# Rebuilding phase one of a fused scan-and-attention kernel: fused rotations, carry on GpSimd, sums on TensorE, V ahead, states in x's memory

## The chip, the cores and the metric

The kernel runs on one core of a Trainium2 chip. The metric is device time in microseconds (us); lower is better. An execution is called slow if it takes more than 1.5% longer than the fastest one of the same kernel. A profiled execution gives a trace whose span is about 1.7 us shorter than the time of the same run. Times below are medians of runs; spans and waits come from the one profiled execution.

Engine names as in the profile: PE is TensorE (PEld its weight loads), DVE is VectorE, ACT is ScalarE, POOL is GpSimd, SP is SyncE, which here mainly issues DMAs. The suffix q (SPq, ACTq) marks a DMA issued from that engine. PSUM is the memory into which the matmuls here write; evacuation is the copying of a finished result out of it. The granted clock is the share of TensorE's full clock that the profile shows; a half-clock window is a stretch in which it is 0.5.

## The reference

Two independent computations on 2048 tokens of 1024 values, whose results stand side by side in the output.

```python
# A: a complex diagonal state space model (1024 states)
Lam_bar = exp(dt * Lam);  B_bar = ((Lam_bar - 1) / Lam)[:, None] * Bmat
Bu = einsum('bld,pd->blp', x, B_bar)
for t in range(L):  h = Lam_bar * h + Bu[:, t, :]          # states h, kept for every t
y = 2 * einsum('blp,dp->bld', hseq, Cmat).real + x * Dskip
# B: attention in 64 segments of 32 tokens, 32 heads of 128, with 8 memory rows
for s in range(n_seg):
    h = concatenate([mem, x[segment s]])
    q, k, v = h @ Wq, h @ Wk, h @ Wv
    o = softmax(mask(q k^T * scale)) v;   o = o @ Wo
    mem = o[:8];  out(o[8:])
return concatenate([y, out], -1)
```

The kernel evaluates B from a guess of the memory rows. The guess needs the sum of x over each segment.

## The kernel before

Phase one goes through 8 chunks (`pc`) of 128 states and, for each, four quarters (`tb`) of 512 tokens. Each quarter has 32 matmuls of the projection V = x Wv (`v_x`) and 16 matmuls of B x (`stage1`), all with 512 columns. The scan is made real by rotating the products by a table of cosines and sines, scanning real and imaginary part separately, and rotating back. The states go to DRAM (`a_hs`). Phase two multiplies the states by C (`stage2`) and computes the memory guess. Phase three is attention and its output projection.

```python
def stage1(self, pc, tb):
    tcp, tsp, tc2, ts2 = self.tabs
    ur = k.ps("S"); ui = k.ps("O")
    for i, u in enumerate((ur, ui)):
        for c in range(KC):
            PE.matmul(u[:], self.bt[:, i, c, :], self.xT[:, c, tb * TB:(tb + 1) * TB], start=(c == 0), stop=(c == KC - 1))
    # rotation: six VectorE operations on 512 columns
    V.tensor_tensor(wr[:], ur[:], c_, ALU.mult)
    V.tensor_tensor(ta[:], ui[:], s_, ALU.mult)
    V.tensor_tensor(wr[:], wr[:], ta[:], ALU.add)
    # ... the same three for wi
    V.tensor_tensor_scan(wr[:], rb, wr[:], 0.0 if ini is None else ini[:, 0:1], ALU.mult, ALU.add)
    V.tensor_tensor_scan(wi[:], rb, wi[:], 0.0 if ini is None else ini[:, 1:2], ALU.mult, ALU.add)
    if tb < NB - 1:      # carry to the next quarter: four VectorE operations on one column
        V.tensor_scalar(tt[:, 0:1], wi[:, TB - 1:TB], sT, None, ALU.mult)
        V.scalar_tensor_tensor(nx[:, 0:1], wr[:, TB - 1:TB], cT, tt[:, 0:1], ALU.mult, ALU.subtract)
        # ... the same two for nx[:, 1:2]
    S.activation(gr[:], wr[:], ACT.Copy); S.activation(gi[:], wi[:], ACT.Copy)
    # rotation back: six bf16 VectorE operations, into h
    k.SP.dma_start(self.hs[tb][:, pc, :, :], h[:])

def sum_x(self):         # segment sums on VectorE
    # ... for pieces of the transposed x:
    k.V.tensor_reduce(self.xsum[...], self.xe[...].rearrange("p c (s n) -> p c s n", n=SEG), AX.X, ALU.add)

def v_x(self, hb, w):
    # ... 8 matmuls into a PSUM tile, copied by ScalarE to the staging tile st (b_vst, 2 buffers)
    k.SP.dma_start(vx[s0:s0 + n * 128, :]..., st[:, 0:n, :, :]...)

def load_c(self, q):     # called in chunks 4 to 7
    for i, w in enumerate((self.Cre, self.Cim)):
        self.k.SP.dma_start_transpose(self.CT[:, i, :, cols], w[cols, :])

# main loop of phase one
for pc in range(PC):
    v = b.v_x(pc, wv)
    for tb in range(NB):
        # ... in chunk 0: V first, and the next quarters of x loaded
        a.stage1(pc, tb)
        # ... tb == 2: tables and B weights of the next chunk
        # ... pc > 0: four steps of V;  pc >= 1: two steps of sum_x
    if pc >= 2:
        b.og(pc, wv)     # needs the sums; 32 matmuls of 64 columns
# phase two: stage2 loads the states (a_hl) into memory taken after phase one,
#   guess(), and at its very end v_mem(0), v_mem(1): memory rows of V

def qk_init(self, pool): # start of phase three: zero the padding of two pairs of q and k tiles
    for i in range(2):
        # ... three V.memset for each of q and k
```

A scheduler orders the instructions of each engine; a DMA is free to be moved ahead unless it is pinned with `keep_in_program_order`.

Of the kernel before, what the change touches and what calls it, by code (L numbers as in the profile page):

```python
# [51 lines left out]
class K:  # L52
    def __init__(self, tc, ctx):
        self.tc, self.nc = tc, tc.nc
        nc = tc.nc
        self.V, self.G, self.S, self.PE, self.SP = nc.vector, nc.gpsimd, nc.scalar, nc.tensor, nc.sync
        self.cst = ctx.enter_context(tc.tile_pool(name="cst", bufs=1, side="left"))
        self.psp = ctx.enter_context(tc.tile_pool(name="ps", bufs=1, space=PSUM))
        self.drp = ctx.enter_context(tc.tile_pool(name="dr", bufs=1, space=DRAM))

    def ps(self, tag, shape=(128, 512), dt=FP32):
        return self.psp.tile(list(shape), dt, name="ps" + tag, bufs={"P": 3, "S": 2, "R": 1, "O": 2}[tag])
# [8 lines left out]
def consts(k):  # L71
# [6 lines left out]
    k.ones = c.tile([128, 128], BF16, name="ones")  # L78
    V.memset(k.ones[:], 1.0)
    k.hpb = c.tile([128, 1], FP32, name="hpb")  # L80
    V.memset(k.hpb[:], HALF_PI)

# [43 lines left out]
class PartA:  # L126
# [6 lines left out]
    def params(self, pool, tmp):  # L133
# [45 lines left out]
        ji = tmp.tile([128, TB + 1], I32, name="a_k1")  # L179
# [3 lines left out]
    def tables(self, pc):  # L183
        k = self.k; V, S = k.V, k.S
        tp, tb = self.tmp, self.tab
        turn, bre, bim, jf = self.turn, self.bre, self.bim, self.jf
        q = pc % 2
        tcp = tb.tile([128, TB + 1], FP32, name=f"a_tabc{q}", bufs=1); tsp = tb.tile([128, TB + 1], FP32, name=f"a_tabs{q}", bufs=1)
        tc2 = tb.tile([128, TB], BF16, name=f"a_tabd{q}", bufs=1); ts2 = tb.tile([128, TB], BF16, name=f"a_tabe{q}", bufs=1)
        k1 = tp.tile([128, TB + 1], FP32, name="a_k1")  # L190
        V.tensor_scalar(k1[:], jf[:], turn[:, pc:pc + 1], MAGIC, ALU.mult, ALU.add)
        V.tensor_scalar(k1[:], k1[:], MAGIC, None, ALU.subtract)
        fr = tp.tile([128, TB + 1], FP32, name="a_fr")
        V.scalar_tensor_tensor(fr[:], jf[:], turn[:, pc:pc + 1], k1[:], ALU.mult, ALU.subtract)
        S.activation(tsp[:], fr[:], ACT.Sin, scale=TWO_PI_LO)
        V.scalar_tensor_tensor(k1[:], fr[:], -1.0, fr[:], ALU.mult, ALU.max)
        S.activation(tcp[:], k1[:], ACT.Sin, scale=-TWO_PI_LO, bias=k.hpb[:])
        t1 = tp.tile([128, TB + 1], FP32, name="a_k1")
        S.activation(t1[:, 0:TB], tsp[:, 0:TB], ACT.Copy, scale=bim[:, pc:pc + 1])
        V.scalar_tensor_tensor(tc2[:], tcp[:, 0:TB], bre[:, pc:pc + 1], t1[:, 0:TB], ALU.mult, ALU.subtract)  # L200
        t2 = tp.tile([128, TB + 1], FP32, name="a_fr")
        S.activation(t2[:, 0:TB], tcp[:, 0:TB], ACT.Copy, scale=self.nbim[:, pc:pc + 1])
        V.scalar_tensor_tensor(ts2[:], tsp[:, 0:TB], self.nbre[:, pc:pc + 1], t2[:, 0:TB], ALU.mult, ALU.add)
        self.tabs = (tcp, tsp, tc2, ts2)
# [10 lines left out]
    def load_c(self, q):  # L215

        cols = slice(q * 256, (q + 1) * 256)
        for i, w in enumerate((self.Cre, self.Cim)):
            self.k.SP.dma_start_transpose(self.CT[:, i, :, cols], w[cols, :])

    def stage1(self, pc, tb):
        k = self.k; V, S, PE = k.V, k.S, k.PE
        if tb == 0:
            self.carry = None
        tcp, tsp, tc2, ts2 = self.tabs
        ur = k.ps("S"); ui = k.ps("O")
        for i, u in enumerate((ur, ui)):
            for c in range(KC):
                PE.matmul(u[:], self.bt[:, i, c, :], self.xT[:, c, tb * TB:(tb + 1) * TB], start=(c == 0), stop=(c == KC - 1))  # L229
        c_, s_ = tcp[:, 0:TB], tsp[:, 0:TB]  # L230
        wr = self.wp.tile([128, TB], FP32, name="a_wr"); wi = self.wp.tile([128, TB], FP32, name="a_wi")
        ta = self.wp.tile([128, TB], FP32, name="a_ta", bufs=1)
        V.tensor_tensor(wr[:], ur[:], c_, ALU.mult)
        V.tensor_tensor(ta[:], ui[:], s_, ALU.mult)
        V.tensor_tensor(wr[:], wr[:], ta[:], ALU.add)
        V.tensor_tensor(wi[:], ui[:], c_, ALU.mult)
        V.tensor_tensor(ta[:], ur[:], s_, ALU.mult)
        V.tensor_tensor(wi[:], wi[:], ta[:], ALU.subtract)
        rb = self.rr[:, pc:pc + 1].to_broadcast([128, TB])
        ini = self.carry  # L240
        V.tensor_tensor_scan(wr[:], rb, wr[:], 0.0 if ini is None else ini[:, 0:1], ALU.mult, ALU.add)
        V.tensor_tensor_scan(wi[:], rb, wi[:], 0.0 if ini is None else ini[:, 1:2], ALU.mult, ALU.add)
        if tb < NB - 1:
            cT, sT = tcp[:, TB:TB + 1], tsp[:, TB:TB + 1]
            nx = self.wp.tile([128, 2], FP32, name="a_nx"); tt = self.wp.tile([128, 2], FP32, name="a_tt")
            V.tensor_scalar(tt[:, 0:1], wi[:, TB - 1:TB], sT, None, ALU.mult)
            V.scalar_tensor_tensor(nx[:, 0:1], wr[:, TB - 1:TB], cT, tt[:, 0:1], ALU.mult, ALU.subtract)
            V.tensor_scalar(tt[:, 1:2], wi[:, TB - 1:TB], cT, None, ALU.mult)
            V.scalar_tensor_tensor(nx[:, 1:2], wr[:, TB - 1:TB], sT, tt[:, 1:2], ALU.mult, ALU.add)
            self.carry = nx  # L250
        gr = self.wp.tile([128, TB], BF16, name="a_gr"); gi = self.wp.tile([128, TB], BF16, name="a_gi")
        S.activation(gr[:], wr[:], ACT.Copy); S.activation(gi[:], wi[:], ACT.Copy)

        h = self.wp.tile([128, 2, TB], BF16, name="a_h")
        n1 = self.wp.tile([128, TB], BF16, name="a_n1", bufs=1); n2 = self.wp.tile([128, TB], BF16, name="a_n2", bufs=1)
        V.tensor_tensor(n1[:], gr[:], tc2[:], ALU.mult)
        V.tensor_tensor(n2[:], gi[:], ts2[:], ALU.mult)
        V.tensor_tensor(h[:, 0, :], n1[:], n2[:], ALU.add)
        V.tensor_tensor(n1[:], gr[:], ts2[:], ALU.mult)
        V.tensor_tensor(n2[:], gi[:], tc2[:], ALU.mult)  # L260
        V.tensor_tensor(h[:, 1, :], n1[:], n2[:], ALU.subtract)
        k.SP.dma_start(self.hs[tb][:, pc, :, :], h[:])

    def stage2(self, pool):

        k = self.k; V, G, PE = k.V, k.G, k.PE
        q0 = k.G
        dB = pool.tile([128, D], BF16, name="a_dB", bufs=1)
        q0.dma_start(dB[:], self.Dskip.unsqueeze(0).to_broadcast([128, D]))
        xns = {}  # L270

        def load_xn(t, q):
            xns[t] = pool.tile([128, D], BF16, name="a_xn2", bufs=3)
            q.dma_start(xns[t][:], self.x[0][t * 128:(t + 1) * 128, :])
        for t in range(3):
            load_xn(t, q0)

        def load_h(tb, q0):
            hl = []
            for q in range(4):  # L280
                hl.append(pool.tile([128, 2, 2, TB], BF16, name=f"a_hl{q}", bufs=2))
                k.tc.keep_in_program_order(q0.dma_start(hl[q][:], self.hs[tb][:, 2 * q:2 * q + 2, :, :]))
            return hl
        nxt = load_h(0, q0)
        for tb in range(NB):
            hl = nxt
            for tt in range(4):
                t0 = tb * TB + tt * 128
                xn = xns.pop(4 * tb + tt)
                xd = pool.tile([128, D], FP32, name="a_xd", bufs=2)  # L290
                G.tensor_tensor(xd[:], xn[:], dB[:], ALU.mult)
                ot = pool.tile([128, D], BF16, name="a_ot", bufs=2)
                for half in range(2):
                    hs = slice(half * 512, (half + 1) * 512)
                    py = k.ps("O")
                    for pc in range(PC):
                        for i in range(2):
                            PE.matmul(py[:], hl[pc // 2][:, pc % 2, i, tt * 128:(tt + 1) * 128], self.CT[:, i, pc, hs],  # L298
# [3 lines left out]
                k.SP.dma_start(self.out[0, t0:t0 + 128, 0:D], ot[:])  # L302
                if 4 * tb + tt + 3 < TT:
                    load_xn(4 * tb + tt + 3, k.SP)
                if tt == 0 and tb + 1 < NB:
                    nxt = load_h(tb + 1, k.SP)
# [3 lines left out]
class PartB:  # L310
# [20 lines left out]
    def init(self, tmp):  # L331
        k = self.k
        k.V.memset(self.accE[:], 0.0)
        m0 = tmp.tile([M, D], BF16, name="b_m0", bufs=1)
# [9 lines left out]
        z = tmp.tile([32, 4 * EV], BF16, name="b_zero", bufs=1)  # L344
# [8 lines left out]
    def load_x(self, q):  # L353

        for t, c, n in self.chunks(q):
            step = 128 if q == 0 else n
            for o in range(0, n, step):
                self.k.SP.dma_start_transpose(self.xe[:, :, c + o:c + o + step], self.x[0][t + o:t + o + step, :])
# [7 lines left out]
    def sum_x(self):  # L366

        k = self.k
        for t, c, n in sum((self.chunks(q) for q in range(4)), []):
            m = 2 if n > 64 else KC  # L370
            for h in range(0, KC, m):
                k.V.tensor_reduce(self.xsum[:, h:h + m, t // SEG:(t + n) // SEG],
                                  self.xe[:, h:h + m, c:c + n].rearrange("p c (s n) -> p c s n", n=SEG), AX.X, ALU.add)
                yield

    def fin_xbar(self, tmp):
        k = self.k
        ms = tmp.tile([128, KC], FP32, name="b_ms", bufs=1)
        k.V.tensor_reduce(ms[:], self.m0T[:], AX.X, ALU.add)
        k.V.tensor_scalar(self.xbar[:], self.xsum[:], 1.0 / L, None, ALU.mult)  # L380
        k.V.tensor_tensor(ms[:], ms[:], self.xsum[:, :, 0], ALU.add)
        k.V.tensor_scalar(self.xbar[:, :, 0], ms[:], 1.0 / L, None, ALU.mult)

    def load_wv(self, hb):
# [655 lines left out]
```

## Time and profile before

| | before |
|---|---|
| device time, median (lowest to highest) | 1290.06 us (1287.63 to 1290.8), 3 runs |
| profiled span, mean granted clock | 1290.2 us, 0.994 |
| phase one / two / three, from the timeline of PE | 363.9 / 134.9 / 791.4 us |

The page begins with the span and the busy time of each engine, its share of the span and its instructions:

```profile
span 1290.2 us, 19225 instructions
PE 1252.3 (97%) x7698; PEld 649.9 (50%) x7698; DVE 716.2 (56%) x1611; ACT 250.7 (19%) x609; POOL 223.7 (17%) x340
```

TensorE is busy 97% of the time, so a faster kernel must win gaps and slow stretches. The share of VectorE, 56%, is an average over phases with different limits. The busy time of each engine in stretches of phase one, followed by the granted clock, the DMA share and GB/s, shows how near VectorE is to its limit:

```profile
60.00:150.00 90.00, 85.22 (x386) 37.74 (x384) 89.76 (x172) 32.93 (x58) 1.35 (x8) 0.99 0.66 161
150.00:250.00 100.00, 100.00 (x546) 46.80 (x545) 93.83 (x183) 37.74 (x67) 1.53 (x9) 1.00 0.41 114
```

The third figure after the length is VectorE: 89.76 us of 90, then 93.83 of 100. GpSimd, the fifth, is all but idle. What PE waits for (in all, how often, longest):

```profile
PE psP L400 <- DMA b_xe<-in_B_x_dram: 12.6, 4, 7.9
PE psP L400 <- ACT b_vst L66: 4.7, 6, 2.9
PE psO L298 <- DMA a_hl<-a_hs: 4.4, 2, 3.8
PE psO L298 <- DVE a_ot L300: 2.7, 3, 2.0
PE psO L563 <- DMA b_v<-b_vt: 2.0, 1, 2.0
```

The first line is the load of x at the start, the second VectorE's backlog in phase one (ScalarE's evacuation waits behind it), the third and fourth phase two, the last phase three. Some VectorE groups by shape, with count, busy time and mean ns:

```profile
L233 DVE TENSOR_TENSOR a_wr<-psS,a_tabc 128x512 f32<-128x512 f32 x32 | 22.0, 686 | 2.0 <-PE psS L229 1.5
L372 DVE TENSOR_REDUCE b_xsum<-b_xe 128x32 f32<-128x1024 bf16 x12 | 14.5, 1213 | 4.0 <-DMA b_xe<-in_B_x_dram 4.0
L256 DVE TENSOR_TENSOR a_n<-a_gr,a_tabd 128x512 bf16<-128x512 bf16 x32 | 12.8, 401 | 0.0
L247 DVE SCALAR_TENSOR_TENSOR a_nx<-a_wr,a_tabc,a_tt 128x1 f32<-128x1 f32 x24 | 5.2, 217 | 0.0
```

These are a multiply of the rotation (0.69 us), a piece of the segment sums (1.2 us), a multiply of the back-rotation (0.40 us) and an operation of the carry on one column (0.22 us; a carry has four, so 0.84 us).

### The profile page before, as it was taken

To read this page: it belongs to the slowest core of one execution; us is meant where nothing else is said; L and a number is where in the kernel's file an instruction comes from. 1 tells how busy PE (TensorE), PEld (TensorE's weight loads), DVE (VectorE), ACT (ScalarE), POOL (GpSimd) and SP (SyncE) were. 2 spreads that over 40 slices of the span, in tenths; PEclk is the share of its full clock that TensorE was granted. 3 is DMA by queue.
4 is the path that set the end of the run, shared out by engine and by line. 5 is a ranking of instruction groups with operands and counts; after the bars stand their busy time and mean duration, and the time that the engine had idled before them with its cause. 6 is when DMAs were issued, how large, how long until landed. Compare 5 with 4: busy or idle time off the path is not lost. (4 is left out here: it accounts for less than half of the span.)

```text
span 1290.2 us, 19225 instructions
## 1 busy us (share of the span) xinstructions
PE 1252.3 (97%) x7698; PEld 649.9 (50%) x7698; DVE 716.2 (56%) x1611; ACT 250.7 (19%) x609; POOL 223.7 (17%) x340
## 2 busy tenths in 40 slices
PE   6899899999989999999999999999999999999997
PEld 2344344444444555556555555565555554444443
DVE  6999999988831123566666665666666641001000
ACT  3333343333310000111112121221211210001000
POOL 7000000000032230222222222222222220000000
PEclk9999999999999999999999999999999999999999
DMA  9994433442399816645464453646464289315000
GB/s 230 244 229 123 123 90 107 123 123 84 98 283 321 261 58 202 120 102 136 102 138 107 102 134 75 147 93 142 96 139 94 62 216 235 72 37 126 17 25 18
DMA packets 312645, 168.88 MB, mean 131 GB/s; under 512 B 140616, under 2 KB 300160, under 8 KB 312552
## 3 DMA queue, kind: packets, MB, share of 16 engines
q1 hardware_dynamic: 310824, 163.91, 51.8%
q0 software_dynamic: 1664, 3.68, 0.9%
q8 instruction: 62, 1.02, 0.3%
q14 instruction: 31, 0.25, 0.1%
q10 hardware_dynamic: 64, 0.02, 0.0%
HBM read 81.18 MB, written 52.19 MB: 103 GB/s over the span
## 5 line engine op out<-in xcount | busy, mean ns | idle before, releaser
L400 PE MATMUL psP<-b_wv,b_xe 128*128 128x512 bf16 x1024 | 232.1, 384 | 17.4 <-DMA b_xe<-in_B_x_dram 12.6
L518 PE MATMUL psP<-b_xe,b_wk 128*128 128x480 bf16 x1024 | 224.1, 367 | 0.0
L518 PE MATMUL psP<-b_xe,b_wq 128*128 128x480 bf16 x1024 | 223.1, 366 | 0.0
L549 POOL TENSOR_TENSOR b_m<-b_e,maskB 99x396 bf16<-99x396 bf16 x160 | 139.6, 873 | 342.1 <-ACT b_e L546 342.1
L546 ACT ACTIVATE b_e<-psS 99x396 bf16<-99x396 f32 x176 | 88.2, 501 | 553.8 <-PE psS L543 549.6
L400 PEld LDWEIGHTS <-b_xe 128*128 128x128 bf16 x1024 | 100.6, 99 | 142.3 <-DMA b_xe<-in_B_x_dram 14.3
L68 DVE CAST b_k<-psP 128x480 bf16<-128x480 f32 (+1 forms) x192 | 98.2, 533 | 101.3 <-PE psP L518 96.8
L68 DVE CAST b_q<-psP 128x480 bf16<-128x480 f32 (+1 forms) x192 | 98.2, 533 | 94.7 <-PE psP L518 92.9
L518 PEld LDWEIGHTS <-b_wk 128*128 128x128 bf16 x1024 | 98.0, 98 | 96.4 <-issue 1.0
L518 PEld LDWEIGHTS <-b_wq 128*128 128x128 bf16 x1024 | 96.7, 98 | 88.0 <-issue 0.2
L642 PEld LDWEIGHTS <-b_ol 128*128 128x128 bf16 x832 | 81.3, 98 | 98.0
L298 PE MATMUL psO<-t,a_hl 128*128 128x512 bf16 x512 | 116.1, 387 | 7.1 <-DMA a_hl<-a_hs 4.4
L68 DVE CAST b_ost<-psP 128x512 bf16<-128x512 f32 x16 | 11.1, 692 | 185.2 <-PE psP L642 185.2
L66 ACT ACTIVATE b_vst<-psP 128x512 bf16<-128x512 f32 x128 | 74.4, 590 | 100.6 <-PE psP L400 76.0
L642 PE MATMUL psP<-wo,b_ol 128*128 128x512 bf16 x416 | 92.4, 379 | 0.0
L642 PE MATMUL psP<-t,b_ol 128*128 128x512 bf16 x416 | 92.2, 379 | 0.0
L566 DVE TENSOR_TENSOR b_ob<-psO,b_accR 99x384 bf16<-99x384 f32 x160 | 86.0, 554 | 2.5
L298 PEld LDWEIGHTS <-a_hl 128*128 128x128 bf16 x512 | 49.9, 99 | 68.4 <-issue 6.9
L300 DVE TENSOR_TENSOR a_ot<-psO,a_xd 128x512 bf16<-128x512 f32 x32 | 21.9, 691 | 107.1 <-PE psO L298 79.5
L229 PEld LDWEIGHTS <-a_bt 128*128 128x128 bf16 x512 | 49.7, 98 | 62.0 <-issue 1.9
L543 PEld LDWEIGHTS <-b_k 128*128 128x128 bf16 x704 | 50.2, 98 | 34.2 <-issue 0.5
L229 PE MATMUL psS<-a_xT,a_bt 128*128 128x512 bf16 x256 | 60.5, 379 | 2.4 <-DMA a_xT<-in_A_x_dram 2.4
(201 smaller groups left out, 1149.6 us busy)
## 6 DMA issues: line engine op xcount, KB each, us to landing
b_v<-b_vx SPq DMA_DIRECT2D x16, 1064.2 KB
b_wv<-in_B_Wv_dram SPq DMA_DIRECT2D x16, 1024.0 KB
b_on<-b_ob SPq DMA_DIRECT2D x15, 960.0 KB
b_vx<-b_vst SPq DMA_DIRECT2D x24, 516.0 KB
a_hs<-a_h SPq DMA_DIRECT2D x32, 256.0 KB
b_wq<-in_B_Wq_dram SPq DMA_DIRECT2D x16, 512.0 KB
b_wk<-in_B_Wk_dram SPq DMA_DIRECT2D x16, 512.0 KB
b_wog<-in_B_Wo_dram SPq DMA_DIRECT2D x4, 2048.0 KB
```

What stands on the lines that cost most here:

```text
L66: self.S.activation(out, in_, ACT.Copy)
L68: self.V.tensor_copy(out, in_)
L229: PE.matmul(u[:], self.bt[:, i, c, :], self.xT[:, c, tb * TB:(tb + 1) * TB], start=(c == 0), stop=(c == KC - 1))
L298: PE.matmul(py[:], hl[pc // 2][:, pc % 2, i, tt * 128:(tt + 1) * 128], self.CT[:, i, pc, hs], start=(pc == 0 and i == 0), stop=(pc == PC - ...
L300: V.tensor_tensor(ot[:, hs], py[:], xd[:, hs], ALU.add)
L400: k.PE.matmul(p[:], self.xe[:, c, t * 128:(t + 1) * 128], w[:, c, :], start=(c == 0), stop=(c == KC - 1))
L518: PE.matmul(p[:, 0:480], w[i][:, c, hh * 128:(hh + 1) * 128], self.xe[:, c, 480 * q:480 * q + 480], start=(c == 0), stop=(c == KC - 1))
L543: PE.matmul(s[:, gg, hh, :], kt[:, hh, g0:g0 + 128], qt[:, hh, g0:g0 + GW], start=True, stop=True)
L546: k.S.activation(e[:], s[0:GW], ACT.Exp, scale=float(E) ** -0.5, accum_out=self.accE[0:GW, i:i + 1])
L549: k.G.tensor_tensor(m[:, 0:4 * GW].rearrange("p (a b q) -> p a b q", a=2, b=2), e[:], mask[0:GW, :, :].unsqueeze(2).to_broadcast([GW, 2, 2 ...
L566: V.tensor_tensor(self.ob[:, b0:b0 + n, :], o[0:GW, 0:n, 0:E], r.unsqueeze(2).to_broadcast([GW, n, E]), ALU.mult)
L642: self.k.PE.matmul(p[:], ol[h][:, tt * 128:(tt + 1) * 128], self.wo[half][:, h, :], start=(h == 0), stop=(h == H - 1))
```

## The change

The intent is to take work off VectorE in phase one, to have its results ready sooner for phase two, and to shorten the start.

```diff
 def stage1(self, pc, tb):
+    u = k.ps("U", (128, 2, TB))                        # real and imaginary part in one two-bank PSUM tile
+    V.tensor_tensor(pr[:], u[:].unsqueeze(1).to_broadcast([128, 2, 2, TB]),
+                    view(t3, [[TB + 1, 2], [TB + 1, 2], [1, TB]]), ALU.mult)   # all four products
+    V.tensor_tensor(w, w, pr[:, :, 1, :], ALU.add)     # both sums
     # ... two scans and two ScalarE casts as before, into g
     # ... (tables(): three tables in one tile; a part of the work on them moved from VectorE to ScalarE)
     if tb < NB - 1:
-        # four VectorE operations
+        for j in range(2):
+            G.tensor_scalar(tt[:, j:j + 1], w[:, j, TB - 1:TB], t3[:, 1, TB:TB + 1], None, ALU.mult)
+            G.tensor_scalar(nx[:, j:j + 1], w[:, 1 - j, TB - 1:TB], t3[:, 2 - 2 * j, TB:TB + 1], None, ALU.mult)
+        G.tensor_tensor(nx[:], nx[:], tt[:], ALU.add)
-    # six bf16 operations of 512 columns
+    V.tensor_tensor(n[:], g[:].unsqueeze(1).to_broadcast([128, 2, 2, TB]), view(r3, [[TB, 2], [TB, 2], [1, TB]]), ALU.mult)
+    V.tensor_tensor(h[:], n[:, :, 0, :], n[:, :, 1, :], ALU.add)

 def sum_x(self, tmp):
-    # VectorE reductions over the transposed x
+    def load(t):     # rows of x, 3 buffers
+        k.tc.keep_in_program_order(k.G.dma_start(xrs[t][:], self.x[0][t * 128:(t + 1) * 128, :]))
+    # ... for each of 16 blocks of 128 tokens:
+        for c in range(KC):
+            k.PE.matmul(p[:, o:o + 4], xr[:, c * 128:(c + 1) * 128], k.ind[:], start=True, stop=True)
+        load(t + 3)

 # phase one
+    warm(k, p1)                                         # 10 matmuls on zeros
+    # ... smaller first loads, all x transposes issued at the start
+    FIRST = [("v", 0), ("v", 1), ("s", 0), ("v", 2), ("s", 1), ("v", 3), ("s", 2), ("s", 3)]   # order in chunk 0
+    LAST = MID[:5] + [("s", 3), ("v", 2), ("v", 3)]     # order in chunk 7: V behind the last scan
-    k.SP.dma_start(vx[...]...)                          # stores of V
+    k.nc.scalar.dma_start(vx[...]...)
 # phase two
+    # ... s2_tiles: state tiles lie where xT was, so they load before phase one is over
-            k.SP.dma_start(self.out[0, t0:t0 + 128, 0:D], ot[:])
+            k.nc.scalar.dma_start(self.out[0, t0:t0 + 128, 0:D], ot[:])
+    # ... v_mem(0), v_mem(1) moved from the end of phase two to its steps 27 and 29
+    # ... (phase three: the next pair's V loaded at u == 2 instead of u == 0)
```

(The two fused multiplies have stride-0 broadcasts of the left operand and overlapping views of three tables on the right.)

## The prediction

> **What bounds it now.** TensorE. The page gives PE 97% of 1290.2 us; VectorE has 56%, but 92-100% up to 300 us (busy time by stretch). Back to back, 32 matmuls of 512 columns start 6.91 us apart (timeline), 0.216 us each; only gaps and slow stretches can be won. By the PE timeline:
>
> - Phase one ends at 363.9 us. Its 1536 wide matmuls (331.5 us), six guess blocks (5.6) and small ones need 338 us, so 26 us are lost: 7.9 us until the first transposed tokens land; some 12 us of load-bound gaps and cold matmuls up to 60.7 us, when the first of eight chunks is through; about 8 us at 105-150 us, where VectorE also does the segment sums (19.7 us) and the evacuation of V waits behind it (4.7 us, list of waits). After the last, 2.9 us, 8 matmuls took 3.27 us instead of 1.89.
> - Phase two, 363.9 to 498.8 us, needs 124: 11 us lost, namely 3.85 + 0.57 us for the states' load, 2.7 us for VectorE freeing PSUM, and about 4 us of slow matmuls (half-clock windows, matmuls dribbling in as states land).
> - Attention and output: 791 us, lost only 1.97 us for the memory rows of V and one half-clock window (about 1.7 us).
>
> Such windows are in the Trainium skill, "TensorE: Matmul & The Clock Gate", Part 1: half clock after an idle window of about 3.4 us. The trace agrees: mean clock 0.87 in 140-150 us.
>
> **What the change does.**
> - VectorE: per stage1 tile 16 operations become 6. Before: 4x0.687+2x0.675, scans 2x1.28, 6x0.42, carry 0.84 = 10 us. After, by the Trainium skill, "VectorE: DVE Perf Modes", perf-mode tier table (bf16 tensor_tensor 1.22 us at 2048 elements; fp32 2.29; the trace agrees at 512: 0.42 and 0.69): 2.29+1.2+2.56+1.22+0.69 = 8 us. Per chunk, with tables, about 35 us against PE's 41.4 (before 43). VectorE stops binding.
> - TensorE gains 128 small sum matmuls; at the 29 ns of the 64-column ones (32 in 0.93 us) 3.7 us. Their loads queue on GpSimd behind the carry, which waits for scans: I expect two or three stalls, about 3 us.
> - Start: smaller first loads, 10 warming matmuls, V ahead; still load-bound (about 235 GB/s, 8 MB transposed): first chunk through at about 56 instead of 60.7 us, held by the next B weights behind the last x transpose.
> - States land early over x, with 64 V matmuls (13.8 us) behind the last scan matmuls: phase two about 125.5 instead of 135 us.
> - Memory V rows come earlier: the 1.97 us wait and its half-clock window go, -3.7 us.
>
> **Sum (estimates).** Start -4.7; later phase one -7.5+1 left, +3.7+3; phase two -9.5; attention -3.7. About -18 to -20 us: **1271 us**, 80% range **1263 to 1279**. Faster by over 2%: 0.13; within 2%: 0.85; slower: 0.02.
>
> **What would show it.** Right: VectorE under 90% in 100-350 us; fused multiply 2.3 us (PSUM) and 1.2 us (bf16); phase one ending near 359; no wait on states over 1 us; no half-clock window after 60 us; attention and output near 787.5 us.
>
> **What would make it wrong.** Broadcast bf16 multiply at single rate (2.3 us): VectorE binds again. Stalls on sum loads long enough for half clock. Heavier early loading in phase two (about 26 MB in 125 us) making states or output weights late. Better: transposes landing sooner than at 235 GB/s, which would approach 1262.

## The result, and the profile after

| | before | after |
|---|---|---|
| device time, median (lowest to highest), 4 runs each | 1290.43 us (1287.63 to 1293.66) | 1307.98 us (1305.81 to 1311.47) |
| profiled span, mean granted clock | 1290.2 us, 0.994 | 1304.1 us, 0.986 |
| phase one / two / three | 363.9 / 134.9 / 791.4 us | 382.7 / 124.6 / 796.8 us |

The ratio of after to before is 1.0138, with a 95% interval of 1.0104 to 1.0171. A ratio here and below is the mean time of one kernel's fast runs over that of the other's of the same rounds, so it is not quite the ratio of the medians quoted. The change made the kernel slower, by less than 2%, and the time lies well outside the predicted range.

The three phases account for the whole difference of the spans (+18.8 - 10.4 + 5.4 = +13.9 us, after rounding). The page after:

```profile
span 1304.1 us, 19165 instructions
PE 1256.0 (96%) x7766; PEld 654.9 (50%) x7836; DVE 665.9 (51%) x1234; ACT 265.0 (20%) x633; POOL 295.0 (23%) x443
```

The stretches of phase one:

```profile
60.00:150.00 90.00, 72.88 (x414) 33.49 (x421) 63.73 (x59) 31.41 (x54) 24.30 (x43) 0.89 0.74 182
150.00:250.00 100.00, 99.47 (x511) 46.40 (x519) 79.11 (x67) 39.48 (x70) 20.52 (x35) 1.00 0.36 113
```

VectorE was indeed relieved: 79 us of 100 instead of 94. But between 60 and 150 us TensorE is busy for 72.9 us instead of 85.2, and its clock is 0.89 instead of 0.99. The list of PE's waits tells for what:

```profile
PE psR L387 <- DMA b_xr<-in_B_x_dram: 12.4, 5, 7.5
PE psP L558 <- DVE b_q L70: 5.1, 1, 5.1
PE psU L240 <- DVE a_pr L242: 4.9, 1, 4.9
PE psU L240 <- DMA a_xT<-in_A_x_dram: 3.9, 1, 3.9
```

The costliest is the wait of the sum matmuls for the rows of x (`b_xr`). The waits of phase two are gone; that phase became 10.4 us shorter. A new wait of 5.1 us stands at the beginning of phase three. The wait of 4.9 us put down to VectorE is in truth one for the B weights, as the wait of the weight loads there shows:

```profile
PEld L240 <- DMA a_bt<-in_A_B_re_dram: 5.4, 1, 5.4
```

The timeline around the longest stall, on the engines involved (start, duration, what, and in brackets the idle time before it with its releaser):

```profile
84.36 0.53 SPq L263 DMA_DIRECT2D a_hs<-a_h  x1
...
88.36 0.69 DVE L262 TENSOR_TENSOR a_h<-a_n 128x1024 bf16<-128x1024 bf16 x1 [2.97 <-DMA a_hs<-a_h]
88.97 2.45 DVE L250 TENSOR_TENSOR_SCAN a_pr<-a_rr,a_nx,a_pr 128x512 f32<-128x512 f32 x2
...
90.34 1.16 POOL L255 TENSOR_SCALAR a_tt<-a_pr,a_tabf 128x1 f32<-128x1 f32 x1 [8.48 <-DVE a_pr L250]
91.48 3.87 POOL L256 TENSOR_SCALAR a_nx<-a_pr,a_tabf 128x1 f32<-128x1 f32 x2
...
95.69 0.20 POOL L257 TENSOR_TENSOR a_nx<-a_nx,a_tt 128x2 f32<-128x2 f32 x1
96.17 1.66 POOL L378 DMA_DIRECT2D b_xr<-in_B_x_dram  x3 [0.29 <-issue]
...
99.20 0.38 PE L387 MATMUL psR<-ind,b_xr 128*128 128x4 bf16 x8 [7.46 <-DMA b_xr<-in_B_x_dram]
...
102.16 8.75 PE L419 MATMUL psP<-b_wv,b_xe 128*128 128x512 bf16 x30 [0.22 <-issue]
```

Read from the bottom: TensorE sat idle 7.46 us until rows of x landed. GpSimd issued their loads at 96.17, having come out of the carry only at 95.9; the carry took from 90.34 on, 5.5 us instead of the 0.84 us it takes on VectorE. The carry had waited 8.48 us for the scan, and the scan stood behind an operation that itself waited 2.97 us for an earlier state store to be done. Afterwards 30 matmuls took 8.75 us; at the pace of 32 in 6.91 us they need 6.5.

The groups behind this, with count, busy time and mean ns:

```profile
L242 DVE TENSOR_TENSOR a_pr<-psU,a_tabf 128x2048 f32<-128x2048 f32 x32 | 73.2, 2288 | 40.1 <-PE psU L240 40.1
L261 DVE TENSOR_TENSOR a_n<-a_g,a_tabh 128x2048 bf16<-128x2048 bf16 x32 | 39.2, 1224 | 29.6 <-ACT a_g L251 29.6
L255 POOL TENSOR_SCALAR a_tt<-a_pr,a_tabf 128x1 f32<-128x1 f32 x48 | 35.5, 740 | 241.2 <-DVE a_pr L250 241.2
L257 POOL TENSOR_TENSOR a_nx<-a_nx,a_tt 128x2 f32<-128x2 f32 x24 | 19.6, 816 | 2.0
L256 POOL TENSOR_SCALAR a_nx<-a_pr,a_tabf 128x1 f32<-128x1 f32 x48 | 16.9, 365 | 0.0
```

The fused multiplies cost what was predicted. The last three lines are the carry on GpSimd: its operations on one or two columns cost 0.74, 0.82 and 0.37 us on average.

At the beginning of phase three:

```profile
508.22 0.34 ACTq L305 DMA_DIRECT2D out_dram<-a_ot  x1
...
515.74 0.10 DVE L517 MEMSET b_q<- 128x50 bf16 x1 [7.21 <-DMA out_dram<-a_ot]
...
516.93 3.38 PE L558 MATMUL psP<-b_xe,b_wq 128*128 128x480 bf16 x8 [5.08 <-DVE b_q L70]
```

The zeroing of the second pair of q and k tiles, at the head of VectorE's work, waits for the last store of part A's output, whose tile had the same memory. The evacuation of q stands behind it in VectorE's order, and TensorE runs out of PSUM.

### The profile page after: what moved, and what is told of

Same layout as the page of the kernel before. It is cut to its first block, busy times and chain, and to the rows that moved or that the text cites. A ratio compares the mean times of both kernels' runs of the same rounds, so it can differ in the third digit from the quotient of the medians.

```text
span 1304.1 us, 19165 instructions
## 1 busy us (share of the span) xinstructions
PE 1256.0 (96%) x7766; PEld 654.9 (50%) x7836; DVE 665.9 (51%) x1234; ACT 265.0 (20%) x633; POOL 295.0 (23%) x443
## 3 DMA queue, kind: packets, MB, share of 16 engines
q8 instruction: 63, 1.03, 0.3%
## 5 line engine op out<-in xcount | busy, mean ns | idle before, releaser
L240 PE MATMUL psU<-a_xT,a_bt 128*128 128x512 bf16 x492 | 118.5, 389 | 9.8 <-DVE a_pr L242 4.9
L301 PE MATMUL psP<-t,a_hl 128*128 128x512 bf16 x497 | 112.0, 379 | 0.8
L70 DVE CAST b_ost<-psP 128x512 bf16<-128x512 f32 x16 | 11.1, 692 | 185.2 <-PE psP L682 184.2
L242 DVE TENSOR_TENSOR a_pr<-psU,a_tabf 128x2048 f32<-128x2048 f32 x32 | 73.2, 2288 | 40.1 <-PE psU L240 40.1
L255 POOL TENSOR_SCALAR a_tt<-a_pr,a_tabf 128x1 f32<-128x1 f32 x48 | 35.5, 740 | 241.2 <-DVE a_pr L250 241.2
```

The costliest lines, as they stand in the source:

```text
L70: self.V.tensor_copy(out, in_)
L240: PE.matmul(u[:, i, :], self.bt[:, i, c, :], self.xT[:, c, tb * TB:(tb + 1) * TB], start=(c == 0), stop=(c == KC - 1))
L242: V.tensor_tensor(pr[:], u[:].unsqueeze(1).to_broadcast([128, 2, 2, TB]), view(t3, [[TB + 1, 2], [TB + 1, 2], [1, TB]]), ALU.mult)
L255: G.tensor_scalar(tt[:, j:j + 1], w[:, j, TB - 1:TB], t3[:, 1, TB:TB + 1], None, ALU.mult)
L301: PE.matmul(py[:], self.hl[tb % 2][pc // 2][:, pc % 2, i, tt * 128:(tt + 1) * 128], self.CT[:, i, pc, hs], start=(pc == 0 and i == 0), sto ...
```

## The experiments

All experiments start from the changed kernel and undo or alter a part of it. All gave correct results. In four batches, each on one chip, the kernel before ran alongside: medians 1289.36, 1290.47, 1289.79 and 1290.55 us. Since batches ran on different chips, the ratio to the kernel before is what is compared across batches; the changed kernel itself was run only in the first measurement, so every gain over it is such a comparison.

| run | edit to the changed kernel | median us (lowest to highest) | ratio to before [95%] |
|---|---|---|---|
| the changed kernel | none | 1307.98 (1305.81 to 1311.47) | 1.0138 [1.0104, 1.0171] |
| e1_carry_dve | carry on VectorE | 1295.60 (1287.89 to 1297.90) | 1.0027 [0.9991, 1.0063] |
| e2_sums_dve | segment sums on VectorE | 1287.49 (1287.16 to 1287.63) | 0.9983 [0.9965, 1.0001] |
| e3_b_early | B weights of chunk 1 loaded early | 1308.29 (1306.56 to 1310.39) | 1.0151 [1.0130, 1.0171] |
| e4_memset_pool | second q, k pair zeroed by GpSimd | 1300.62 (1299.14 to 1303.47) | 1.0093 [1.0070, 1.0116] |
| e5_c_late | C transposes pinned to their place | 1303.13 (1302.70 to 1306.76) | 1.0097 [1.0075, 1.0119] |
| e6_carry_c | e1 + e5 | 1288.33 (1286.17 to 1293.48) | 0.9997 [0.9965, 1.0029] |
| e7_sums_mem | e2 + e4 | 1283.92 (1280.16 to 1285.27) | 0.9940 [0.9912, 0.9967] |
| e8_sums_mem_c | e2 + e4 + e5 | 1279.19 (1277.59 to 1281.92) | 0.9909 [0.9885, 0.9932] |
| e9_ccm | e1 + e4 + e5 | 1279.16 (1278.05 to 1282.01) | 0.9920 [0.9900, 0.9940] |
| e10_ccm_interleaved | e9, V not ahead | 1278.25 (1276.94 to 1280.32) | 0.9907 [0.9887, 0.9926] |
| e11_ccm_no_warm | e9, no warming matmuls | 1279.51 (1276.52 to 1283.58) | 0.9914 [0.9890, 0.9938] |
| e12_all_vector | e1 + e2 + e4 + e5 | 1274.42 (1274.07 to 1275.92) | 0.9880 [0.9861, 0.9899] |
| e13_unfused | e12, rotations in twelve operations | 1280.35 (1277.20 to 1283.55) | 0.9915 [0.9888, 0.9942] |
| e14_all_vector_c_early | e12 without e5 | 1280.91 (1278.84 to 1284.72) | 0.9924 [0.9896, 0.9952] |

The theory, called A: the slow carry on GpSimd delays the loads of the sum rows, which stand behind it in program order on the same engine, and TensorE stalls on them. Rivals and additions: the sums as such cost too much (S); the state stores held back by C transposes on SyncE are the origin (C); the order of the first loads is to blame for the gap at the B weights (B), or the start is bound by the amount of data and the gap only moves (D); the wait at phase three is a matter of the zeroing (M).

### e1_carry_dve: the carry back on VectorE

```diff
-    for j in range(2):
-        G.tensor_scalar(...); G.tensor_scalar(...)
-    G.tensor_tensor(nx[:], nx[:], tt[:], ALU.add)
+    cT = t3[:, 1, TB:TB + 1]
+    for j in range(2):
+        V.tensor_scalar(tt[:, j:j + 1], w[:, 1 - j, TB - 1:TB], t3[:, 2 - 2 * j, TB:TB + 1], None, ALU.mult)
+        V.scalar_tensor_tensor(nx[:, j:j + 1], w[:, j, TB - 1:TB], cT, tt[:, j:j + 1], ALU.mult, ALU.add)
```

> The changed kernel, but the carry of the scan is computed on VectorE again (4 small operations), so GpSimd has only the loads for the segment sums in its queue. Theory A (these loads come late because in GpSimd's queue they stand behind carries that wait for scans): TensorE's waits for b_xr fall from 12.4 us to under 1.5 us, the half-clock windows near 86 and 130 us go, time falls by 12 to 16 us to about 1294. Rival B (the loads are late because the C transposes and state stores fill the transfer engines): waits for b_xr stay above 8 us and the time falls by under 4 us.

The wait for the sum rows fell from 12.4 to 1.7 us, as A says. But a new wait of 7.6 us for ScalarE's evacuation appeared, which no theory had. (The profile is of the slowest of four runs that spread over 10 us, 1287.89 to 1297.90. The half-clock windows that were expected to go stood at 96 and 141 us in the trace; both are gone, and a new one of 6.8 us stands at 101 us, behind the new wait.) The timeline shows its origin on SyncE and VectorE:

```profile
68.88 0.53 SPq L263 DMA_DIRECT2D a_hs<-a_h  x1
...
69.79 0.68 DVE L262 TENSOR_TENSOR a_h<-a_n 128x1024 bf16<-128x1024 bf16 x1
...
84.21 8.20 SPq L229 DMA_TRANSPOSE t<-in_A_C_im_dram  x1
92.45 2.94 SPq L229 DMA_TRANSPOSE t<-in_A_C_re_dram  x1
95.50 0.53 SPq L263 DMA_DIRECT2D a_hs<-a_h  x1
...
99.69 0.69 DVE L262 TENSOR_TENSOR a_h<-a_n 128x1024 bf16<-128x1024 bf16 x1 [14.57 <-DMA a_hs<-a_h]
```

Between 68.88 and 95.50 us SyncE issued no state store, only a V weight load and transposes, four of them of C. The result that was ready at 70.5 us had its store issued only at 95.50. VectorE stood still for 14.57 us because both buffers of its result were waiting to be stored. The C weights are not needed before phase two, and the program asks for them in chunks 4 to 7; the scheduler had moved them to 60-100 us. It did so in the kernel before too (58.6 to 88.4 us in its trace), where VectorE was behind and no such wait is in its list. So A holds, and the C transposes are a second cause, hidden behind the first (tested in e5, e6 and e14).

### e2_sums_dve: segment sums back on VectorE

```diff
-    for t in range(TT):   # loads of xr on GpSimd, 8 matmuls each
+    k.V.tensor_reduce(xsum[:, h:h + m, t // SEG:(t + n) // SEG],
+                      self.xe[:, h:h + m, c:c + n].rearrange("p c (s n) -> p c s n", n=SEG), AX.X, ALU.add)
```

> The changed kernel, but the segment sums are made on VectorE from the transposed x as before: no sum loads, no 128 small matmuls; the carry stays on GpSimd. Theory A: the 12.4 us of waits for b_xr, about 2.6 us of half clock after them and the 3.25 us of small matmuls all go: 16 to 19 us faster, about 1290. Rival C (VectorE still has no room for the sums, which was the reason for moving them): waits of TensorE for VectorE and ScalarE come back in chunks two and three, and under half of that is won.

This one edit takes back the whole loss: 0.9983, an interval that just includes 1, although 14.5 + 3.8 + 1.4 us of reductions return to VectorE. Phase one ends at 365.1 us instead of 382.7. The carry stays on GpSimd here, slow as it is. The slow carry is therefore harmful mainly because loads stand behind it that TensorE waits for. What S says about cost as such is small: 24 of the sum matmuls took 0.61 us (start to the next start), so 128 take 3.3 us by that pace, against some 20 us gained.

### e3_b_early: B weights of chunk 1 before the last x

```diff
                 a.load_x(q)
                 if q < 2:
                     b.load_x(q + 2)
+                if q == 1:
+                    bt0 = a.bt; a.load_b(1); bt1, a.bt = a.bt, bt0
```

> The changed kernel, but the two transposed loads of the second chunk's B weights are issued before the last two x transposes instead of after them. Theory A (the 4.9 us gap at 59 us, with its half-clock window, is the wait for these weights): the gap falls under 1 us and 5 to 7 us are won, about 1302. Rival D (the gap is the two-bank PSUM tile that VectorE's fused multiply frees late, as the list of waits names it): the gap stays above 3 us and the time stays within 2 us.

No gain: 1.0151 against 1.0138. The wait at the B weights is gone from the list, but the waits for the transposed x grew from 3.9 to 10.0 us, the longest, 4.9 us, at 62.5 us. So B fell, and D agrees with the run: the order of the loads moves the gap; the amount of data that must land before about 60 us stays. No run loaded less data, so D itself was not put to the test.

### e4_memset_pool: zeroing off VectorE's queue

```diff
         for i in range(2):
+            V = self.k.G if i else self.k.V
```

> The changed kernel, but the zeroing of the second pair of q and k tiles is done by GpSimd instead of VectorE at the start of attention. Theory A (that zeroing waits 7.2 us for the last store of part A to leave, and VectorE's queue holds up the evacuation that TensorE then waits 5.1 us for): the 5.1 us gap at 512 us and its half-clock window go, 5 to 7 us faster, about 1302. Rival E (the evacuation would be late anyway, or the masks on GpSimd now hold TensorE up): a gap of 3 us or more stays between 507 and 540 us.

The wait at phase three is gone, and with it a window of half clock. Phase three took 788.8 us by the trace (1297.4 - 508.6) instead of 796.8; the time fell by 7.4 us in the medians, and phase one stayed as slow as it was (end at 384.0). M is settled: the zeroing was what made TensorE wait. What it cost is 8.0 us by the traces of phase three, and 5.8 us by the ratios, whose intervals overlap.

### e5_c_late: C transposes where the program has them

```diff
-            self.k.SP.dma_start_transpose(self.CT[:, i, :, cols], w[cols, :])
+            self.k.tc.keep_in_program_order(self.k.SP.dma_start_transpose(self.CT[:, i, :, cols], w[cols, :]))
```

> The changed kernel, but the eight transposed loads of C stay where the program has them (chunks five to eight) instead of being moved by the scheduler in front of the state stores at 59 to 90 us. Theory B in its pure form (the sum loads are late because transfers are congested by C): waits for b_xr fall from 12.4 us to under 3 us and the time by 12 us or more. Theory A (the loads stand behind carries in GpSimd's queue): the 3.0 us wait of VectorE for the state store goes and the longest b_xr wait falls from 7.5 to about 4 us, but waits for b_xr stay at 5 to 9 us in total; 3 to 7 us faster.

Alone it brought about 5 us, by the medians and by the ratios: 1.0097, an interval that overlaps the changed kernel's. The wait for the sum rows stayed, 10.8 us, the longest 6.0. So C is not the origin of that wait; with e1 and e2, what is left is the carry in front of the loads.

### e6_carry_c: both e1 and e5

```diff
+    # the edit of e1 (carry on VectorE) and the edit of e5 (C transposes pinned)
```

> Carry on VectorE as in the first experiment, and the C loads late as well. Theory A plus store order (with the sum loads free, the rest of the loss was VectorE waiting 14.6 us for a state store behind five C transposes in SyncE's queue, and through ScalarE TensorE waiting 7.6 us for PSUM): no wait of TensorE over 2 us between 65 and 380 us, 8 to 11 us faster than the first experiment, about 1286. If C's transposes were not the cause of the late store, the 7.6 us wait stays and the time is within 2 us of 1295.6.

Together they remove the wait for the sum rows and the one for the evacuation: neither is in the list of PE's waits any more. The time is that of the kernel before, 0.9997, and phase one ends at 365.2. Sums on TensorE and the carry on VectorE get along once the state stores flow. Against e1 the time tells less than the waits: 8 to 11 us were expected, and it is 7 by the medians and 4 by the ratios, whose intervals overlap. The 5.0 us wait of phase three is still in this run.

### e7_sums_mem and e8_sums_mem_c: repairs added up

```diff
+    # e7: the edits of e2 (sums on VectorE) and e4 (zeroing);  e8: those and e5 (C transposes pinned)
```

> Segment sums on VectorE (as in the second experiment) and the zeroing on GpSimd (as in the fourth). If the two losses are separate, their gains add: 20.5 + 7.4 us below 1308, about 1280, and the 5.2 us wait for b_q goes. If the first hid part of the second, it stays above 1284.

> As the run before, and the C loads late as well. Theory A with store order: the waits for b_vst (3.2 us) in chunks two and three come from stalls of VectorE or ScalarE and not from SyncE's queue, so little is left to win: 0 to 4 us faster, 1277 to 1280. If the early C transposes slow the loads of B weights and V weights for chunks two and three, 4 us or more.

e7 came to 1283.92 us instead of the 1280 expected: its list has waits of 7.3 us for ScalarE's evacuation. With the C transposes pinned as well (e8) they are 3.0 us, and the time is 1279.19: 4.7 us less by the medians and 4.0 by the ratios, on the border between the two things expected of e8, so it doesn't decide between them. Both beat the kernel before.

### e9_ccm, e10_ccm_interleaved, e11_ccm_no_warm: what the rebuilt start is worth

```diff
+    # e9: the edits of e1, e4 and e5; sums stay on TensorE
 # e10, on top of e9
-FIRST = [("v", 0), ("v", 1), ("s", 0), ("v", 2), ("s", 1), ("v", 3), ("s", 2), ("s", 3)]
+FIRST = [(x, q) for q in range(4) for x in "vs"]     # and one quarter of x loaded less far ahead
 # e11, on top of e9
-            warm(k, p1)
```

> The three separate repairs together: carry on VectorE, C loads late, second zeroing on GpSimd; segment sums stay on TensorE. Theory A with store order and the zeroing: the 5.0 us wait for b_q that stayed in the sixth run goes and the time is 6 to 8 us under that run's 1288.3, about 1281 (ratio to before 0.991 to 0.995). If the gains don't add, it stays above 1285.

> As the run before, but V does not run ahead of the scan in the first chunk: V and scan quarters alternate, with the loads in that order, as in the kernel before. If running 1024 tokens of V ahead hides load time, this is 3 us or more slower. If the first 60 us are bound by the same bytes in any order (the third run moved the gap from one load to another), it stays within 2 us.

> As the run before the last, but without the ten warming matmuls on zeros. If the warming is worth what it was added for, V's first 32 matmuls run at half clock and the time rises by 2 to 4 us. If the first stretch is bound by loads, the lost clock hides under them and the time stays within 2 us.

The three do not differ measurably: 0.9920, 0.9907 and 0.9914. V ahead of the scan (with its order of loads) and the warming matmuls are worth nothing measurable here. This agrees with D: in the first 60 us the DMA engines move 237 GB/s before the change, 242 after and 236 in e12 (stretches), whatever the order in which TensorE uses what lands.

### e12_all_vector: all of it, and the best kernel

```diff
+    # the edits of e1, e2, e4 and e5: carry and sums on VectorE, zeroing on GpSimd, C transposes pinned
     # kept from the change: fused rotations, two-bank PSUM tiles, states on xT's memory, start, early v_mem
```

> Sums and carry both back on VectorE, C late, zeroing on GpSimd: of the relief for VectorE only the fused operations are left. If the fused operations alone give VectorE enough room (about 8.8 us per tile with the carry, 38 us per chunk with tables against TensorE's 41.4), it is within 3 us of the eighth run's 1279.2. If VectorE is too full with the 19.7 us of sums in chunks one to three, waits for b_vst and PSUM of 5 us or more appear there and it is above 1284.

1274.42 us, ratio 0.9880 (0.9861 to 0.9899): faster than both kernels, and 4.8 us faster than the 1279.2 expected (3.7 by the ratios). Its list of PE's waits begins:

```profile
PE psU L240 <- DMA a_bt<-in_A_B_re_dram: 4.3, 1, 4.3
PE psU L240 <- DMA a_xT<-in_A_x_dram: 3.0, 1, 3.0
PE psP L409 <- DMA b_xe<-in_B_x_dram: 1.7, 1, 1.7
```

These fall in the first 65 us. The stretches:

```profile
60.00:150.00 90.00, 87.05 (x411) 39.53 (x420) 86.99 (x106) 40.14 (x71) 0.00 (x0) 0.96 0.42 116
150.00:250.00 100.00, 99.53 (x511) 46.38 (x519) 85.95 (x102) 41.23 (x73) 0.00 (x0) 1.00 0.54 142
```

VectorE has everything back that the change had moved off it and is at 86 of 100 us after the first chunks. The fused operations alone had made enough room (e13 undoes them). Phases one, two and three take 361.3, 123.8 and 787.6 us: 2.6, 11.1 and 3.8 us less than before. That is 17.5 us between two profiled runs; by the ratio of all fast runs it is about 15.5 us.

e9 and e12 ran in one batch and differ only in where the sums are made: 1279.16 against 1274.42. Some 3.3 us of that is the time of the sum matmuls on TensorE; the rest is within the spread of e9's runs. e8 and e12 differ only in the engine of the carry, but ran on different chips, and their intervals overlap (0.9885 to 0.9932, 0.9861 to 0.9899); a cost of the carry on GpSimd with no loads behind it is likely but not shown.

### e13_unfused: what the fused operations are worth in the best kernel

```diff
-        V.tensor_tensor(pr[:], u[:].unsqueeze(1).to_broadcast([128, 2, 2, TB]), view(t3, ...), ALU.mult)
-        V.tensor_tensor(w, w, pr[:, :, 1, :], ALU.add)
+        for j in range(2):
+            for i in range(2):
+                V.tensor_tensor(pr[:, j, i, :], u[:, i, :], t3[:, j + i, 0:TB], ALU.mult)
+            V.tensor_tensor(pr[:, j, 0, :], pr[:, j, 0, :], pr[:, j, 1, :], ALU.add)
         # and the same for the bf16 rotation back
```

> The twelfth run's kernel (sums and carry on VectorE, C late, zeroing on GpSimd), but the rotations in twelve operations of 512 elements, as in the kernel before, instead of four fused ones. VectorE then needs about 2 us more per tile (10 instead of 8.8 us with the carry, near 43 us per chunk with tables against TensorE's 41.4) besides the sums. If the fused operations are what gives VectorE room, waits of TensorE for VectorE or ScalarE come back between 65 and 380 us and it is 6 to 14 us slower, 1280 to 1288. If what won was the rest (states early, loads, store order), it stays within 3 us of 1274.4.

1280.35 us, 5.9 us slower than e12 by the medians and 4.5 by the ratios (0.9915 and 0.9880; the batches and chips differ and the intervals just overlap). Summed from the traces, the operations of a tile take 9.85 us on VectorE here and 8.65 in e12, so fusing saves 1.2 us per tile and not the 2 that were expected. The stretches of this run:

```profile
60.00:150.00 90.00, 83.87 (x360) 36.97 (x368) 88.40 (x179) 35.88 (x63) 0.00 (x0) 0.94 0.40 114
150.00:250.00 100.00, 99.53 (x540) 46.84 (x547) 89.00 (x174) 45.03 (x79) 0.00 (x0) 1.00 0.49 132
```

VectorE is at 98% of the first stretch again, and waits for the evacuation of V return (4.5 us in the list, 0.2 in e12). The fused operations pay there, by some 4 to 6 us.

### e14_all_vector_c_early: the C transposes by themselves

```diff
-            self.k.tc.keep_in_program_order(self.k.SP.dma_start_transpose(self.CT[:, i, :, cols], w[cols, :]))
+            self.k.SP.dma_start_transpose(self.CT[:, i, :, cols], w[cols, :])
```

> The twelfth run's kernel, but the C loads where the scheduler moved them, in front of the state stores. If the early C loads cost only where something waits on GpSimd or on sum loads, it stays within 2 us of 1274.4. If they hold up state stores, and VectorE with them, by themselves, a wait of VectorE for a state store of 3 us or more appears at 80 to 105 us, TensorE waits for b_vst after it, and it is 4 to 9 us slower.

1280.91 us: early C transposes cost about 6 us also where nothing else is wrong (6.5 by the medians, 5.7 by the ratios, whose intervals just touch). VectorE waits 2.9 us for a state store at 91 us, which e12 does not; PE waits 3.0 us for the evacuation, and there is a half-clock window more than in e12, at about 122 us of the span.

## Why the prediction was wrong

The prediction was 1271 us, in a range of 1263 to 1279, and the kernel took 1307.98. Point by point:

**"VectorE: per stage1 tile 16 operations become 6", 8 us instead of 10: right.** The fused multiply took 2288 ns from PSUM and 1224 ns in bf16. (By its own sum the prediction has 18 operations before, not 16. Summed from the traces a tile took 9.75 us on VectorE before, with its share of the carry, and 7.94 after.) The Trainium skill, "VectorE: DVE Perf Modes", the perf-mode tier table, gives 2293 ns for fp32 in SBUF, the same 1x rate without a figure for an operand in PSUM, and 1224 ns for bf16 in SBUF; the trace agrees, also for views with a broadcast dimension, which had been named as what could make the prediction wrong. "VectorE stops binding" was right as well: 79 of 100 us, and the wait for the evacuation of V (4.7 us before) is no longer in the list. And e13 shows that fusing is worth some 4 to 6 us in the best kernel.

**"States land early over x … phase two about 125.5": right.** It took 124.6 us, with no wait for states.

**"Their loads queue on GpSimd behind the carry, which waits for scans: I expect two or three stalls, about 3 us": this step failed.** The mechanism was named, and its size was wrong by far: 12.4 us of waits in five stalls, the longest 7.5 us. Two costs were missing from the sum.

- The carry's time on GpSimd. The prediction took its 0.84 us off VectorE and booked nothing for it on GpSimd. There its five operations take 72 us over 24 carries (35.5, 19.6 and 16.9 in the three lines shown: 3.0 us each), and 5.5 us in the case shown; the profile's durations on GpSimd are rough. An estimate of its part: with carries of 0.84 us the loads of the two groups of stalls (8.6 us at 92 to 101 us, 3.8 us at 136 to 141 us) would have been issued 4.7 and 2.1 us earlier. That is 6.8 of the 12.4 us; the rest is the wait for the scans that the prediction named. No run separates the two, as e1 takes the carry off GpSimd altogether; nor did a run keep it there and issue the loads from another queue. The Trainium skill, "GPSIMD Engine Reference", 1. Specifications, says that GpSimd shares its SBUF interfaces with VectorE, with contention when a VectorE instruction has two SBUF inputs or runs in a two-port mode. The trace agrees: of the 120 carry operations, 74 took at most 0.49 us and 46 at least 0.63; for the 46, on average 94% of the time coincides with VectorE operations that read SBUF alone (15% for the 74), and nine in ten end within 0.1 us of the end of a VectorE operation. The operation of 3.12 us at 91.48 ended 0.07 us after the fifth of a row of six such VectorE operations. That they coincide is shown; no run varied the contention alone.
- The half clock after a stall, which the prediction named as a danger but did not count. The Trainium skill, "TensorE: Matmul & The Clock Gate", Part 1, has half clock after an idle window of about 3.4 us. The trace agrees on the half clock, but not on a gap of that length: in the kernel before, such windows follow gaps of 2.0, 2.0 and 2.9 us (400, 520 and 145 us), and another gap of 2.9 us (46 us) has none. In the changed kernel, after the gaps of 4.9, 7.5 and 3.2 us at 59, 92 and 136 us there are half-clock windows of 6.8, 10.2 and 3.4 us, and the groups of 16, 30 and 30 matmuls behind them took 5.8, 8.6 and 7.7 us to the next group instead of 3.5, 6.5 and 6.5 (at 0.216 us each).

All of phase one's loss lies between 59 us, where the first chunk was through 1.8 us earlier than before, and 171 us, where the changed kernel was 18.8 us behind; that is 20.6 us. It adds up: between 60 and 150 us TensorE is idle for 17.1 us instead of 4.8 (12.3 more), and 0.9 us of the gap at 59 lies before that; half clock costs 5.7 us by the groups just given, against 1.4 us in the kernel before (8 matmuls in 3.1 us at 148 us); the sum matmuls take 3.3 us. The sum is 20.8. Undoing either end of the dependency removes the waits for the sum rows. Phase one then ends at 365.1 us in e2, which is most of the loss, and at 375.7 in e1 with its own new wait; with that wait mended (e6) it ends at 365.2.

**"Start -4.7": failed.** The prediction had called the start "still load-bound" and nevertheless booked 4.7 us. The first chunk was through 1.8 us earlier, and the next one lost 4.9 us at once at its B weights. The same step names the hold, "by the next B weights behind the last x transpose", but still put the first chunk at 56 us and nothing after it. e3 shows that another order only moves the gap, e10 and e11 that V ahead and the warming matmuls are worth nothing measurable.

**"Memory V rows come earlier: the 1.97 us wait and its half-clock window go, -3.7 us": the sign was wrong.** The wait for V went. But the V rows' work at the end of phase two had also been the time in which part A's last output was stored. Without it the zeroing of the second q and k pair, on memory of that output, held VectorE for 7.2 us and TensorE for 5.1, plus half clock: +5.4 us. e4 shows the expected gain once that is mended: phase three takes 788.8 us in e4 and 787.6 in e12, where 787.5 was predicted.

**Not foreseen at all: the C transposes.** Moved ahead by the scheduler, they kept SyncE from issuing state stores. The change did not move them (59 to 88 us before, 60 to 90 after). e1 and e14 show the wait. That VectorE meets it only now because it has become fast enough is the likely reason, but not shown: the change also reordered SyncE's queue.

e12, which keeps the fused operations, the placement of the states and the early V rows, is 15.5 us faster than the kernel before by the ratio, 17.5 us by the profiled spans. That this is near the 18 to 20 us that the prediction expected is partly luck: its sum charged 6.7 us for the sums on TensorE and their stalls, which e12 does not pay. Without them it promised 11.2 us in phase one (4.7 at the start, 6.5 later), and e12 won 2.6 there; phases two and three came out as predicted or better. What the changed kernel lost it lost to the two moves off VectorE that the fused operations had already made unnecessary, and to two orders (zeroing, C transposes). Left open are the waits at the start, some 11 us in e12, which may need less data in the first 60 us rather than another order (no run tried it); whether pinning the C transposes would help the kernel before was not run either.

## What to carry to other kernels

Before moving work to an idle engine, ask what stands behind it in that engine's order: a slow operation there costs little until a load that TensorE waits for queues behind it, and then the stall is paid again in half clock. When one part of a change makes an engine fast enough, try the rest of the relief undone; here taking back two of the moves (and mending two orders) turned a loss of 1.4% into a gain of 1.2%. Where a step is taken away at a boundary of phases, look at what its time had been covering, and pin transfers that are needed late so that they don't hold back the stores of now.

## What the Trainium skill lacked or had wrong

- "GPSIMD Engine Reference" has the contention for SBUF with VectorE but no figure for small operations: on one or two columns of 128 rows, 72 of 120 took 0.20 to 0.28 us, and 39 of the 46 that coincide with VectorE's work 1.03 to 1.17 us, up to 3.12 us, against 0.20 to 0.22 us on VectorE. The page's factor of about 2 (4.1 Engine selection) is given for operations with two inputs, and measured there at 2048 elements; a carry took 3.0 us instead of 0.84.
- "DMA: Bandwidth & Descriptors", Issuing engines are not separate DMA queues, says that issuing on several engines saves only the issue time, which is usually small relative to the DMA itself. It has no figure for what a long issue holds up behind it on the same engine. In e1 transposes held SyncE for 1.3 to 8.2 us each while no state store was issued for 26.6 us, and keeping the C transposes out of the way was worth about 6 us (e14 against e12); when a transpose had landed is not in the traces. The page's figures for a transpose's time in the sequencer are for small tiles or from SBUF; none fits a transpose of this size from DRAM.
- "VectorE: DVE Perf Modes" gives the condition of the fast bf16 mode (16-bit, step 1 or -1) but no case of a view whose outer dimensions overlap, as that of the three tables here. It kept the mode: 1224 ns for 2048 elements.
